# A recurrent-memory attention block: output and input projections in four column groups, transposes moved from TensorE to DMA

## The chip, the cores and the metric

The kernel runs on one core of a Trainium2 chip. The time is device time in microseconds (us) for one execution. The same kernel before the change, run on several chips, had medians from 5,003 to 5,043 us, so kernels of different batches are compared through their ratio to the kernel before of the same batch.

## The reference, cut to what matters

It is a forward and backward pass of one block. The attention half is recurrent: 64 segments of 32 rows run one after the other, each with 8 memory rows that the segment before produced.

```python
for s in range(n_seg):                         # 64 segments, serial
    xs = x[:, s*32:(s+1)*32]                   # 32 rows of 448
    h = concatenate([mem, xs])                 # 8 + 32 = 40 rows
    q, k, v = h@Wq, h@Wk, h@Wv                 # 448 -> 16 heads x 256 = 4096
    p = softmax(mask(q@k.T * scale))
    o = (p@v) @ Wo                             # 4096 -> 448
    mem = o[:, :8]                             # the only link to the next segment
    outs.append(o[:, 8:])
...
h  = x + attention(layernorm(x))
h2 = h + swiglu_ffn(layernorm(h))              # 448 -> 1792 -> 448
# outputs: h2 and the gradients of x, mem0, Wq, Wk, Wv, Wo, w_gate, w_up, w_down
```

The gradient runs the same chain backwards. Only the 8 memory rows tie one segment to the next.

## The kernel before

It has five parts in order: the forward chain, the FFN forward and backward, the backward chain, the attention weight gradients, the FFN weight gradients. Instructions of the chains are issued at high priority; other work (called filler below) is placed by the scheduler into the waits of the chain. Each engine then executes its list in that fixed order, and what stands behind a waiting instruction waits as well: in run 3 four transposes that wait for their operand hold up TensorE 16 times, for 65.2 us in all.

In the chains, everything is kept with features on the partitions and the 40 rows of the segment as the moving operand, so every projection is 128 matmuls of 40 columns.

```python
def wpass(W_sb, s):                            # one of V, Q, K; three passes per segment
    for c in range(MC):                        # MC = 32
        for kc in range(KC):                   # KC = 4
            nc.tensor.matmul(o, lhsT=W_sb[:, kc, c*P:(c+1)*P], rhs=hT_roll[:, kc, sl, :], ...)   # 40 columns
# ... forward, output projection of all 40 rows:
for mc in range(KC):
    for c in range(MC):
        nc.tensor.matmul(pO[:, mc*L:(mc+1)*L], lhsT=Wo_sb[:, c, mc*P:(mc+1)*P], rhs=oT[:, c, :], ...)
# ... backward, 384 of them per segment:
for mc in range(KC):
    for (WT, dT) in ((WvT_sb, dvT), (WkT_sb, dkT), (WqT_sb, dqT)):
        for c in range(MC):
            nc.tensor.matmul(pH[0:msz, mc*L:(mc+1)*L], lhsT=WT[:, c, mcols], rhs=dT[:, c, :], ...)
# ... attention weight gradients: gather, then transpose on TensorE, then accumulate in SBUF
for j in range(8):
    nc.tensor.transpose(pt[:, j*P:(j+1)*P], stg[:, c, :], ident[:, :])
# ... cuts: softmax on 40x640, V and dO transposed on TensorE, end of each FFN tile:
nc.vector.tensor_copy(out=dh_b[:, 0:D], in_=dh_t[:])
for kc in range(KC):
    nc.tensor.transpose(pdT[:, kc*P:(kc+1)*P], dh_b[:, kc*P:(kc+1)*P], ident[:, :])
```

## Time and profile before

The median was 5,043.25 us of 16 runs (5,014.49 to 5,046.56). The first fence has lines from the page of the kernel before: the busy time of each engine with its share and instruction count, two rows of the 40 slices (granted TensorE clock in tenths, and DMA share in tenths), and the chain of work that ended last.

```profile
PE 3974.7 (79%) x94152; PEld 3396.5 (68%) x94192; DVE 2129.7 (42%) x4096; ACT 1577.5 (31%) x2696; POOL 397.4 (8%) x809
...
PEclk9888888888888788987888888888888898887979
DMA  5111111211211311115232322322233346465352
...
PE 64%; DVE 11%; ACT 8%; DMA 8%; issue 5%; SPq 2%; ACTq 0%; POOL 0%; DVEq 0%; POOLq 0%
```

TensorE holds 64% of the chain and issues 94,152 matmuls. DMA has room in the chains: its share is 0.17 and 0.30 in the next fence. The next fence is the table of windows of the kernel before, one row for each stretch: its length, then busy time and instruction count of each engine, granted clock, DMA share, GB/s.

```profile
56.00:1671.00 1615.00, 1290.21 (x41284) 1253.51 (x41285) 798.07 (x1506) 510.98 (x816) 90.34 (x236) 0.87 0.17 61
1671.00:2280.00 609.00, 404.14 (x2500) 230.31 (x2528) 308.22 (x560) 192.57 (x326) 43.04 (x103) 0.87 0.21 72
...
2343.00:3950.00 1607.00, 1425.91 (x44100) 1372.13 (x44096) 544.12 (x1105) 461.50 (x802) 157.52 (x305) 0.86 0.30 91
3950.00:4833.00 883.00, 686.36 (x5152) 442.29 (x5152) 444.20 (x843) 374.75 (x676) 69.80 (x128) 0.88 0.50 145
```

These are the forward chain (25.2 us per segment), the FFN, the backward chain (25.1 us per segment) and the attention weight gradients. Last, the timeline of TensorE in one forward segment: start, length, line, operands, count, and in brackets the idle time before with what ended it.

```profile
609.12 0.72 PE L505 MATMUL psh<-ident,P_sb 40*40 40x40 bf16 x16 [4.36 <-DVE P_sb L501]
...
611.72 3.98 PE L525 MATMUL psf<-oT,Wo_sb 128*128 128x40 bf16 x128
615.98 3.35 PE L367 MATMUL psf<-hT_roll,Wv_sb 128*128 128x40 bf16 x128 [0.28 <-DVE hT_roll L530]
```

A pass of 128 narrow matmuls takes 3.35 us, 26 ns each, and the chain pays for each of them.

### The profile page before, as it was taken

The page shows a single profiled execution, that of the slowest core. Times are in us where ns is not written, and L with a number is a line of the kernel's source. Part 1 is how long each engine was busy: PE and PEld are TensorE (multiplying, and loading weights), DVE is VectorE, ACT ScalarE, POOL GpSimd, SP SyncE. Part 2 cuts the span into 40 slices and gives each one's busy share as a digit, 9 for nine tenths or more (in the row PEclk, how much of TensorE's full clock was granted, in tenths as well). Part 3 has the DMA queues.
Part 4 walks back from the last instruction along what each step waited for, and adds up shares of the span by engine and source line. Part 5 has one row for each costly group of instructions (what it writes and reads, how often), then busy time and mean ns, then how long its engine had stood idle before and what let it go on. Part 6 is the DMA issues. An engine that isn't in the chain of part 4 may idle for free.

```text
span 5027.9 us, 201264 instructions
## 1 busy us (share of the span) xinstructions
PE 3974.7 (79%) x94152; PEld 3396.5 (68%) x94192; DVE 2129.7 (42%) x4096; ACT 1577.5 (31%) x2696; POOL 397.4 (8%) x809
## 2 busy tenths in 40 slices
PE   4788878877887577675898888888888787875949
PEld 3777777777777433344888888888888654543525
DVE  3445544544454455552333333333333363644520
ACT  2333333322333333232222222222222434433420
POOL 2000000000000100001011000100010100000000
PEclk9888888888888788987888888888888898887979
DMA  5111111211211311115232322322233346465352
GB/s 164 52 61 60 68 51 61 77 51 51 78 59 50 118 60 58 65 59 167 85 101 89 96 89 90 95 90 89 90 92 92 122 126 167 144 159 171 119 190 94
DMA packets 257044, 477.74 MB, mean 95 GB/s; under 512 B 95008, under 2 KB 145344, under 8 KB 246992
## 3 DMA queue, kind: packets, MB, share of 16 engines
q1 hardware_dynamic: 215872, 307.71, 19.6%
q0 software_dynamic: 40336, 157.14, 9.6%
q8 instruction: 737, 12.08, 1.0%
q14 instruction: 99, 0.81, 0.1%
HBM read 228.30 MB, written 219.13 MB: 89 GB/s over the span
## 4 chain that ended last, share of the span: by engine, by line
PE 64%; DVE 11%; ACT 8%; DMA 8%; issue 5%; SPq 2%; ACTq 0%; POOL 0%; DVEq 0%; POOLq 0%
PE psf L819 15%; PE psf L367 12%; PE psf L962 5%; PE psf L525 5%; PE psf L745 4%; ACT dO_sb L77 4%; PE psf L1015 2%; PE psf L1049 2%; PE psf L689 2%; SPq L978 1%; PE psh L923 1%; PE psf L756 1%; PE psf L797 1%; PE psf L620 1%; PE psf L806 1%
## 5 line engine op out<-in xcount | busy, mean ns | idle before, releaser
L962 PE MATMUL psf<-H_all,ktg 128*128 128x448 bf16 x1920 | 367.4, 354 | 5.8 <-ACT accT L77 5.8
L825 DVE CAST doutT_all<-psf 128x24 bf16<-128x24 f32 x63 | 11.5, 183 | 735.8 <-PE psf L819 735.8
L819 PE MATMUL psf<-dvT,WvT_sb 128*128 128x40 bf16 x8192 | 295.6, 191 | 22.2 <-issue 22.0
L962 PEld LDWEIGHTS <-ktg 128*128 128x128 bf16 x1920 | 188.0, 98 | 180.6 <-issue 8.5
L819 PE MATMUL psf<-dqT,WqT_sb 128*128 128x40 bf16 x8192 | 287.9, 188 | 21.7 <-issue 21.7
L819 PE MATMUL psf<-dkT,WkT_sb 128*128 128x40 bf16 x8192 | 290.2, 189 | 17.6 <-issue 17.4
L819 PEld LDWEIGHTS <-WvT_sb 128*128 128x128 bf16 x8192 | 269.1, 107 | 29.5 <-issue 24.2
L819 PEld LDWEIGHTS <-WqT_sb 128*128 128x128 bf16 x8192 | 264.3, 106 | 24.5 <-issue 24.0
L525 PE MATMUL psf<-oT,Wo_sb 128*128 128x40 bf16 x8192 | 274.3, 198 | 8.3 <-DVE oT L75 3.0
L819 PEld LDWEIGHTS <-WkT_sb 128*128 128x128 bf16 x8192 | 266.5, 106 | 20.3 <-issue 20.0
L525 PEld LDWEIGHTS <-Wo_sb 128*128 128x128 bf16 x8192 | 271.1, 109 | 12.0 <-DVE oT L75 4.2
L77 ACT COPY dO_sb<-psh 40x1024 bf16<-40x1024 bf16 x256 | 238.6, 1007 | 107.5 <-PE psh L776 107.5
L923 PE MATMUL psh<-ident,kstg 128*128 128x128 bf16 x2048 | 160.2, 252 | 131.8 <-DVE kstg L915 131.8
L832 ACT COPY dxnT_tile<-psf 128x96 f32<-128x96 f32 x64 | 15.3, 239 | 778.4 <-DVE doutT_all L826 767.1
L923 PEld LDWEIGHTS <-kstg 128*128 128x128 bf16 x2048 | 151.0, 116 | 141.6 <-DVE kstg L915 139.0
L745 PE MATMUL psf<-doutT_all,WoT_sb 128*128 128x40 bf16 x8192 | 224.2, 182 | 13.1 <-DVE doutT_all L825 13.1
L745 PEld LDWEIGHTS <-WoT_sb 128*128 128x128 bf16 x8192 | 224.3, 98 | 14.0 <-issue 12.0
L367 PE MATMUL psf<-hT_roll,Wk_sb 128*128 128x40 bf16 x8192 | 222.3, 179 | 13.9 <-issue 13.0
L367 PEld LDWEIGHTS <-Wv_sb 128*128 128x128 bf16 x8192 | 216.4, 96 | 17.8 <-issue 17.6
L367 PE MATMUL psf<-hT_roll,Wv_sb 128*128 128x40 bf16 x8192 | 217.5, 180 | 13.5 <-DVE hT_roll L530 13.5
L505 PE MATMUL psh<-ident,P_sb 40*40 40x40 bf16 x1024 | 41.3, 188 | 234.7 <-DVE P_sb L501 234.7
L367 PEld LDWEIGHTS <-Wk_sb 128*128 128x128 bf16 x8192 | 212.4, 96 | 18.4 <-issue 18.0
(293 smaller groups left out, 7224.1 us busy)
## 6 DMA issues: line engine op xcount, KB each, us to landing
VT_all<-vT SPq DMA_DIRECT2D x64, 320.0 KB, 2.2
OT_all<-oT POOLq DMA_DIRECT2D x64, 320.0 KB, 2.8
vT_b<-VT_all SPq DMA_DIRECT2D x64, 320.0 KB, 2.9
dVT_all<-dvT SPq DMA_DIRECT2D x64, 320.0 KB, 2.7
dKT_all<-dkT POOLq DMA_DIRECT2D x64, 320.0 KB, 4.1
dQT_all<-dqT SPq DMA_DIRECT2D x64, 320.0 KB, 4.4
Kx<-tmq SPq DMA_DIRECT2D x64, 256.0 KB, 2.4
Qx<-tmq SPq DMA_DIRECT2D x64, 256.0 KB, 2.4
```

The costliest lines, as they stand in the source:

```text
L77: nc.scalar.copy(out=out, in_=in_)
L367: nc.tensor.matmul(o, lhsT=W_sb[:, kc, c * P:(c + 1) * P], rhs=hT_roll[:, kc, sl, :], start=(kc == 0), stop=(kc == KC - 1))
L525: nc.tensor.matmul(pO[:, mc * L:(mc + 1) * L], lhsT=Wo_sb[:, c, mc * P:(mc + 1) * P], rhs=oT[:, c, :], start=(c == 0), stop=(c == MC - 1))
L620: nc.tensor.matmul(pg[:, 0:f1 - f0], lhsT=hnT[:, kc, :], rhs=Wg_sb[:, kc, f0:f1], start=(kc == 0), stop=(kc == KC - 1))
L689: nc.tensor.matmul(pdh[:, 0:D], lhsT=srcT[:, c, :], rhs=WT[:, c, :], start=(i == 0), stop=(i == nmm - 1))
L745: nc.tensor.matmul(o, lhsT=WoT_sb[:, kc, c * P:(c + 1) * P], rhs=doutT_all[:, kc, s, :], start=(kc == 0), stop=(kc == KC - 1))
L756: nc.tensor.matmul(pdP[b][0:L, hh, 0:L], lhsT=doT[:, c, :], rhs=vT[:, c, :], start=(dc == 0), stop=(dc == DC - 1))
L819: nc.tensor.matmul(pH[0:msz, mc * L:(mc + 1) * L], lhsT=WT[:, c, mcols], rhs=dT[:, c, :], start=(i == 0), stop=(i == 3 * MC - 1))
L923: nc.tensor.transpose(pt[:, j * P:(j + 1) * P], stg[:, c, :], ident[:, :])
L962: nc.tensor.matmul(pacc[:, 0:D], lhsT=KT_sb[:, sl, j * P:(j + 1) * P], rhs=H_all[:, kt, 0:D], start=(i == 0), stop=(i == len(slots) - 1))
L1015: nc.tensor.matmul(pacc[:, 0:D], lhsT=KT_sb[:, sl, mc * P:(mc + 1) * P], rhs=dOut_all[:, kt, :], start=(i == 0), stop=(i == len(slots) - 1))
L1049: nc.tensor.matmul(pacc[:, 0:f1 - f0], lhsT=HN_all[:, kt, mc * P:(mc + 1) * P], rhs=X_all[:, kt, f0:f1], start=(kt == 0), stop=(kt == NT - 1))
```

## The change: intent and diff

The intent is to issue fewer, wider matmuls on the chain. Only the 8 memory rows need the output projection at once; the other 32 rows can wait until four segments make a full 128-row tile. For the 8 rows the roles of the operands are swapped: the activations (32 columns, 8 of them real) are loaded as weights, and the weight matrix streams as 448 columns. Four such matmuls, each writing to its own 32 of the 128 rows of one PSUM tile (a column group), can run side by side. Small FP32 matmuls then add the four partial sums. Most transposes leave TensorE for the DMA (issued from SyncE, SP). Below is the core of the diff, long parts cut.

```diff
-            for mc in range(KC):
-                for c in range(MC):
-                    nc.tensor.matmul(pO[:, mc * L:(mc + 1) * L], lhsT=Wo_sb[:, c, mc * P:(mc + 1) * P],
-                                     rhs=oT[:, c, :], start=(c == 0), stop=(c == MC - 1))
+            pO = k.ps1()
+            for j in range(MC):
+                nc.tensor.matmul(pO[32 * (j % 4):32 * (j % 4) + 32, 0:D], lhsT=oTm[:, j, :], rhs=Wo_sb[:, cj(j), :],
+                                 start=(j < 4), stop=(j >= MC - 4), skip_group_check=True)
+            ...                                          # copy to om, FP32 sum of the four groups by 'sel'
+        if r == 3:                                       # filler: the other rows, once per 128-row tile
+            for j in range(MC):
+                nc.tensor.matmul(px[:, 0:D], lhsT=xblk[:, j, :], rhs=Wo_sb[:, cj(j), :], ...)
... V: x rows projected per tile as filler; the 8 memory rows in column groups on the chain, then copied into V
+            for j in range(4):
+                eng.dma_start(out=Vs[64 * g + SEG:64 * g + L, ...], in_=v_sb[32 * j:32 * j + M, :])
... backward: DMA transposes in place of TensorE's, three projections in column groups, the rest as filler (px)
+        nc.sync.dma_start_transpose(out=vT[...], in_=dr["VG"][s])      # also Q_sb, K_sb: 512 KB each
+            nc.sync.dma_start_transpose(out=dO_sb[:], in_=doT[...])    # on the chain
+                for j in range(MC):
+                    nc.tensor.matmul(pH[32 * (j % 4):32 * (j % 4) + 32, 0:D], lhsT=dm_pad[nm][:, j, :], rhs=WT[:, cj(j), :], ...)
... FFN: the transpose of dh at the end of a tile is gone; dh goes to DRAM and is transposed by DMA later
-        for kc in range(KC):
-            nc.tensor.transpose(pdT[:, kc * P:(kc + 1) * P], dh_b[:, kc * P:(kc + 1) * P], ident[:, :])
... attention weight gradients: transposed tiles by DMA, accumulation over 20 blocks in PSUM
+                    nc.sync.dma_start_transpose(out=x_t[...], in_=src)              # 256 KB each, 320 of them
```

## The prediction

> **What bounds it now.** TensorE, at its instruction rate. The page counts 94,152 matmuls and as many weight loads, PE busy 79% of 5028 us; in the chain of waits PE holds 64%. By the table of windows: prologue 0–56, forward chain 56–1671 (64 serial segments, 25.2 us each), FFN 1671–2280, weight loads to 2343, backward chain 2343–3950 (25.1 us per segment), attention weight gradients 3950–4833 (883 us), FFN weight gradients to 5028. In the timeline 128 matmuls of 40 columns take 3.36 us: 26 ns each. So the chains pay per matmul.
>
> **What changes.** About 53,500 matmuls remain.
> - Forward, per segment: the V pass (3.36 us) and V transposes (1.95) go; V is projected per 128-row tile off the chain, only the 8 memory rows on it (32 matmuls of 512 columns in four column groups). Output projection: 128 narrow matmuls (4.46 us) become 32 of 448 columns in four column groups, memory rows only. Softmax runs on 128x320 instead of 40x640 (0.81 us per op becomes about 0.45). New on the chain: four small SBUF-to-SBUF copies that put the memory rows into V (small DMAs here land in about 1.7–2.2 us), and four FP32 matmuls summing the column groups (about 0.7 us).
> - Backward, per segment: 384 matmuls of the three input projections (about 13.5 us) become 96 wide ones in column groups (about 2 us per 32); dO transposes on TensorE with four ACT copies (3.7 us) become one DMA transpose; 96 narrow head matmuls become 48. Added: four 512 KB DMA transposes per segment on the SP queue.
> - Attention weight gradients: the transposes (2,560 matmuls), the SBUF accumulations and the transposed write-back go; 320 DMA transposes of 256 KB feed PSUM accumulation over 20 blocks.
>
> Everything rests on column groups running concurrently.[...]
>
> **Sum (estimates from the durations above).** Forward segment: two passes 6.75, evacuation and scores 1.0, softmax and V evacuation 2.8, DMA 2.7, PV 1.2, projection 2.0, FP32 sum and copies 1.5: with semaphores 18.8 us. Backward segment: pass 3.95, scores and softmax 3.3, three rounds of about 3.1 us, sum and copies 1.5, filler 1.3: about 20 us; SP needs about 9 us of it for transposes, hidden. Weight gradients: 1,440 matmuls of 512 columns at 0.216, 480 in pairs, 640 of 448 at 0.19, plus bubbles: about 560 us. The SP queue issued 1 MB transposes every 4.2 us, so 84 MB takes about 355 us, hidden.
> 70 + 64x18.8 + 605 + 63 + 64x20 + 560 + 195 = about 3,980; with DMA contention I say 4,020 us, 8 in 10 between 3,750 and 4,400. Faster by over 2%: 0.94; within 2%: 0.02; slower: 0.04.
>
> **What would show each step.** 32 column-group matmuls spanning about 2 us (6–7 us if serial: then near 5,200 us and slower). Segments of 18–20 us forward, 19–21 backward. In the forward chain, the small V copies as the releaser before PV. In the gradient stretch PE, not SP, as limiter; 30–35 us per quarter.
>
> **What would make it wrong.** Column groups serialising; the small V copies waiting behind the 512 KB stores of Q, K, V; DMA transposes of 256–512 KB slower than the 1 MB ones, making the SP queue the limit in the backward chain or the gradients.

A speed-up was assumed for four column groups; no trace showed it at the time. No term is missing from the sum, which came to about 3,980 us, and 4,020 with contention, but the terms of about 2 us for 32 column-group matmuls rest on that assumption: the projection's 2.0 us forward and the three backward rounds, 3.1 us each with their other parts. From the trace of before one can only bound them: matmuls of 448 columns start 189 ns apart, so 32 take 6.0 us one after the other and 1.5 us if four run wholly side by side (estimates). The changed kernel and run 2 give the answer: 1.70 us in four groups, 6.23 in one. The pairing of 480 matmuls in the weight gradients was assumed too; in the changed kernel the second of a pair starts 3 to 4 ns after the first (L887). Two smaller estimates: the softmax operations on VectorE came out at 0.49 us ("about 0.45"), and the FP32 sum on TensorE, with filler between, at 1.26 us from start to end ("about 0.7"; medians).

## The result and the profile after

The changed kernel took 4,024.46 us (median of 9 runs, 4,015.51 to 4,049.9) against 5,043.25 us; the ratio is 0.7991, 95% interval 0.7974 to 0.8007. The predicted 4,020 us is nearly exact, but the stretches show that this is in part luck. First the page of the changed kernel, the lines that answer to those shown of before.

```profile
PE 3314.0 (82%) x54269; PEld 2086.0 (52%) x54366; DVE 1413.6 (35%) x3195; ACT 871.7 (22%) x2021; POOL 816.8 (20%) x1733
...
PEclk9999989999998799886899999999999888999979
DMA  7334334333333312218788888868887799999852
```

The matmuls fell to 54,269, and DMA is now busy: the backward chain and the attention weight gradients are at 8 and 9 tenths. (The chain of work that ended last covers only 10% of this trace, so it is not used for the changed kernel.) The table of windows of the changed kernel, stretch for stretch:

```profile
57.00:1306.00 1249.00, 1104.57 (x26011) 798.19 (x26066) 510.13 (x1153) 331.42 (x782) 235.85 (x535) 0.93 0.39 142
1306.00:1838.00 532.00, 385.03 (x2412) 223.81 (x2440) 294.74 (x548) 182.67 (x317) 49.13 (x119) 0.89 0.22 80
...
1906.00:3164.00 1258.00, 1155.12 (x22522) 752.74 (x22521) 484.40 (x1216) 271.66 (x783) 369.48 (x824) 0.95 0.81 168
3164.00:3834.00 670.00, 526.76 (x2594) 237.85 (x2592) 99.80 (x230) 72.40 (x111) 125.23 (x201) 0.89 1.03 193
```

| stretch (us) | before | predicted | after |
|---|---|---|---|
| prologue | 56 | 70 | 57 |
| forward chain, 64 segments | 1,615 | 1,203 | 1,249 |
| FFN | 609 | 605 | 532 |
| weight loads | 63 | 63 | 68 |
| backward chain, 64 segments | 1,607 | 1,280 | 1,258 |
| attention weight gradients | 883 | 560 | 670 |
| FFN weight gradients | 195 | 195 | 197 |

The chains gave 715 of the 997 us saved between the two profiled runs (366 forward, 349 backward). The attention weight gradients gave 213 where 323 were expected; the FFN gave 77 where 4 were. The timeline of TensorE in two neighbouring forward segments of the changed kernel shows what the main part of the gain looks like, and something the prediction did not have:

```profile
917.04 1.23 PE L451 MATMUL psf<-PT_bd,V 128*128 128x80 bf16 x16 [2.20 <-DMA V<-v_sb]
918.20 2.67 PE L461 MATMUL psf<-Wo_sb,oTm 128*32 128x448 bf16 x32
...
934.36 2.44 PE L493 MATMUL fx<-Wo_sb,xblk 128*128 128x448 bf16 x12
936.64 0.74 PE L451 MATMUL psf<-PT_bd,V 128*128 128x80 bf16 x16
937.44 1.70 PE L461 MATMUL psf<-Wo_sb,oTm 128*32 128x448 bf16 x32
```

L461 is the projection in column groups: 32 matmuls of 448 columns (a set, below) in 1.70 us. In the trace the four matmuls of a round start within 11 ns of each other, and the rounds 0.18 to 0.19 us apart. L451 is the product of the probabilities and V (PV, below). In the segment before, where TensorE stood idle for 2.20 us first, the same 32 took 2.67 us; where filler (L493) ran instead, they took 1.70. L451 shows the same, 1.23 against 0.74. The windows of the two sets show the granted clock, third figure from the end:

```profile
918.20:920.87 2.67, 2.67 (x35) 1.11 (x34) 0.69 (x2) 0.79 (x3) 0.94 (x2) 0.62 0.77 308
937.44:939.14 1.70, 1.70 (x33) 0.84 (x34) 0.72 (x2) 0.79 (x3) 0.94 (x2) 1.00 0.67 258
```

In segments 1 to 62 of the forward chain it was 1.00 in each of the 37 sets that took 1.70 us, and 0.50 to 0.64 in each of the 25 that took longer.

What TensorE waited for in the changed kernel, from the list of waits (total us, times, longest):

```profile
PE psf L883 <- ACT wres L77: 58.3, 9, 31.2
PE psf L714 <- DMA dO_sb<-doT: 56.5, 17, 7.5
...
PE psf L451 <- DMA V<-v_sb: 44.4, 25, 2.2
```

Apart from one of the FFN that the kernel before has as well (58.3 us, 16 times, for VectorE's dgp), these are the three largest waits that recur: evacuations (copies of TensorE's results out of their PSUM tiles) in the attention weight gradients, the transpose of dO (the gradient of PV's result) in the backward chain, the copies of V's memory rows in the forward chain. Each was tried.

### The profile page after: what moved, and what is told of

It reads as the page before. It is cut to its first block, busy times and chain, and to the rows that moved or that the text cites. A ratio compares the mean times of both kernels' runs of the same rounds, so it can differ in the third digit from the quotient of the medians.

```text
span 4031.1 us, 121412 instructions
## 1 busy us (share of the span) xinstructions
PE 3314.0 (82%) x54269; PEld 2086.0 (52%) x54366; DVE 1413.6 (35%) x3195; ACT 871.7 (22%) x2021; POOL 816.8 (20%) x1733
## 5 line engine op out<-in xcount | busy, mean ns | idle before, releaser
L883 PE MATMUL psf<-xt,HC 128*128 128x512 bf16 x1440 | 349.6, 405 | 112.7 <-ACT wres L77 58.3
L883 PEld LDWEIGHTS <-HC 128*128 128x128 bf16 x1440 | 146.9, 103 | 314.2 <-issue 167.4
L723 PE MATMUL psf<-do_roll,WoT_sb 128*128 128x40 bf16 x8192 | 218.4, 180 | 74.1 <-POOL do_roll L683 72.3
L379 PEld LDWEIGHTS <-Wq_sb 128*128 128x128 bf16 x8192 | 228.9, 99 | 19.6 <-issue 8.2
L379 PE MATMUL psf<-hT_roll,Wq_sb 128*128 128x40 bf16 x8192 | 229.5, 184 | 6.6 <-DVE hT_roll L473 5.3
L414 PE MATMUL psf<-Wv_sb,memT_pad 128*32 128x512 bf16 x2048 | 147.7, 381 | 0.4 <-issue 0.3
L461 PE MATMUL psf<-Wo_sb,oTm 128*32 128x448 bf16 x2048 | 142.0, 433 | 2.9 <-DVE oTm L75 0.4
L794 PE MATMUL fx<-WqT_sb,blkq 128*128 128x448 bf16 x512 | 128.5, 365 | 0.0
L794 PE MATMUL fx<-WvT_sb,blkv 128*128 128x448 bf16 x512 | 127.8, 369 | 0.0
L842 DVE COPY mpk<-mld 128x1024 bf16<-128x1024 bf16 x32 | 13.4, 434 | 324.9 <-DMA xt<-mpk 277.6
L794 PE MATMUL fx<-WkT_sb,blkk 128*128 128x448 bf16 x512 | 124.6, 354 | 0.0
```

Of the source, the lines that this page charges most:

```text
L379: nc.tensor.matmul(pss[b][:, jj * L:(jj + 1) * L], lhsT=W_sb[:, kc, c * P:(c + 1) * P], rhs=hT_roll[:, kc, sl, :], start=(kc == 0), stop=( ...
L414: nc.tensor.matmul(pV[b][32 * j:32 * j + 32, 0:512], lhsT=memT_pad[:, kc, :], rhs=Wv_sb[:, kc, n * 512:(n + 1) * 512], start=(kc == 0), st ...
L461: nc.tensor.matmul(pO[32 * (j % 4):32 * (j % 4) + 32, 0:D], lhsT=oTm[:, j, :], rhs=Wo_sb[:, cj(j), :], start=(j < 4), stop=(j >= MC - 4), ...
L723: nc.tensor.matmul(pss[b][:, jj * L:(jj + 1) * L], lhsT=WoT_sb[:, kc, c * P:(c + 1) * P], rhs=do_roll[:, kc, sl, :], start=(kc == 0), stop ...
L794: nc.tensor.matmul(px[:, 0:D], lhsT=blk[nm][:, j, :], rhs=WT[:, cj(j), :], start=(wi == 0 and j == 0), stop=(wi == 2 and j == MC - 1))
L883: nc.tensor.matmul(pa[2 * kc + g][:, 0:512], lhsT=HC[:, b, kc * P:(kc + 1) * P], rhs=xt[b][:, :, g, :], start=(b == 0), stop=(b == NB - 1))
```

## The experiments

Twelve kernels were run, in four batches with the kernel before in each. In the traces of the experiments the forward stretch is counted to the first TensorE instruction of the FFN, because that is easy to find in every trace; so counted it is 1,274 us in the changed kernel, 25 us more than in the table above. For parts of the kernel that an experiment left untouched, the stretches repeat from trace to trace within these limits (seven traces or more each): forward 1,271 to 1,278 us, backward 1,226 to 1,258, attention weight gradients 654 to 684. A difference inside such limits shows nothing.

### 1. Column groups one after the other, first attempt

```diff
-            for j in range(MC):
+            for j in sorted(range(MC), key=lambda j: (j % 4, j)):      # also in the backward chain
```

> The changed kernel, but the 32 matmuls of the memory-row projections (one projection forward, three backward, per segment) are issued one column group after the other instead of going round the four groups. Same count, same shapes, same sums. My theory: the gain comes from four column groups running at once; 32 matmuls, now 1.70 us in the trace, then span about 6 us[...], +4.3 us four times in each of 64 segments, so about +1,100 us and a time near 5,100 us. Rival: what counts is only that 128 or 96 narrow matmuls became 32 wide ones (fewer instructions); then the order is indifferent and the time stays within 1% of 4,024 us.

It took 4,542.13 us, ratio 0.9053 (0.899 to 0.9116), correct. So the order of the groups alone is worth about half of the gain. But a set spanned 4.00 us, not 6.0 (32 times the 189 ns from start to start in the kernel before), at the same granted clock of 1.00. From the trace: in one set, the first four and the last four matmuls start 0.189 us apart, those between start in pairs, the second of a pair 0.005 to 0.017 us after the first. Two groups still ran side by side, so the experiment did not do quite what it was meant to.

### 2. All 32 matmuls in one column group

```diff
-                nc.tensor.matmul(pO[32 * (j % 4):32 * (j % 4) + 32, 0:D], ...
-                                 start=(j < 4), stop=(j >= MC - 4), ...)
+                nc.tensor.matmul(pO[0:32, 0:D], ...
+                                 start=(j == 0), stop=(j == MC - 1), ...)
... the same for pH in the backward chain; only om[0:32] is copied, the other rows stay zero
```

> All 32 memory-row matmuls of a set (one set forward, three backward per segment) add into column group 0 alone, so no two of them can run side by side; the order question of the first attempt is gone and the result stays correct. Theory (the column groups run concurrently, and this is what pays for the change): each set spans [...]6.0 us instead of 1.70, 4.3 us per segment forward and 12.9 backward, 64 segments: +1,100 us, about 5,120 us, ratio 1.02 to the kernel before, so the whole gain is gone. Rival (the 4.00 us of the first attempt was already serial, and the rest was accumulation into one bank): 4.0 us per set again, about 4,540 us.

It took 5,069.33 us, ratio 1.0091 (1.0047 to 1.0135), correct. The timelines of TensorE, one line of the first attempt and one of this kernel, are:

```profile
903.84 4.00 PE L461 MATMUL psf<-Wo_sb,oTm 128*32 128x448 bf16 x32
```

```profile
901.84 6.23 PE L461 MATMUL psf<-Wo_sb,oTm 128*32 128x448 bf16 x32
```

With little else changed (the copies of the sums read 32 rows instead of 128), 32 matmuls take 6.23 us in one group and 1.70 us in four, both at a granted clock of 1.00: 3.7 times. In one group they start 189 ns apart, as the full-width matmuls of 448 columns in the changed kernel do, so adding up in one place costs nothing extra. The forward stretch grew by 285 us and the backward stretch by 750, and the whole kernel is no faster than the kernel before. The theory holds: without concurrency of the column groups the change gains nothing in sum. Counted as in the table above, the forward chain would be about 1,534 us (1,615 before) and the backward chain 2,008 (1,607); the other parts keep their gains. The rival (4.0 us was already serial) is out.

### 3. The FFN's transposes put back

The FFN gained 77 us though the change only drops four transposes per tile there.

```diff
+        pdT = ps1(BF16)
+        for kc in range(KC):
+            nc.tensor.transpose(pdT[:, kc * P:(kc + 1) * P], dh_b[:, kc * P:(kc + 1) * P], ident[:, :])
+        dhT = work.tile([P, KC, P], BF16, name="dhT", bufs=1)
+        k.evac(dhT[:], pdT[:, 0:KC * P].rearrange("p (c n) -> p c n", n=P))
```

> The changed kernel, with the four TensorE transposes of the layer-norm gradient put back at the end of each of the 16 FFN tiles (and their copy out of PSUM, into a scratch tile nobody reads). Theory: in the FFN the in-order TensorE waited 4.1 us per tile for the vector chain that ends in this tile (61 us in the trace of before); the FFN stretch goes from 532 back to about 600 us, the time from 4,024 to about 4,090 us. Rival: the FFN gained for another reason (its loads, its PSUM pool, the strided copy into the persistent gradient tile); then only the work itself comes back, 64 short matmuls, 7 us, and the time stays under 4,040 us.

It took 4,076.31 us, ratio 0.8136 (0.8096 to 0.8176), correct; the FFN stretch grew by 61 us. The waits of TensorE, the line in the kernel before and the line that came back:

```profile
PE psh L701 <- DVE dh_b L697: 65.3, 16, 4.1
```

```profile
PE psh L652 <- DVE dh_b L647: 65.2, 16, 4.1
```

The four transposes need dh, the last result of VectorE's chain of layer-norm operations. In TensorE's fixed order they stood before the next tile's matmuls and held them up to 4.1 us, 16 times. Once they start, the four take 0.40 us in this trace, so nearly all of the 61 us is the wait, not the work.

### 4. Filler taken out of the forward chain

```diff
-            for j in range(MC):
-                nc.tensor.matmul(px[:, 0:D], lhsT=xblk[:, j, :], rhs=Wo_sb[:, cj(j), :], start=(j == 0), stop=(j == MC - 1))
+            for j in range(1):
+                nc.tensor.matmul(px[:, 0:D], lhsT=xblk[:, j, :], rhs=Wo_sb[:, cj(j), :], start=True, stop=True)
```

> Wrong on purpose: the forward output projection per 128 rows, which runs between the chain's matmuls on the same in-order engine, is cut from 32 matmuls of 448 columns to 1, 16 times in the forward stretch (96 us of PE work over all: 31 x 0.19 x 16). Theory (fillers stretch the serial chain, because a chain matmul that becomes ready must wait for the filler already in the queue): the forward stretch loses 40 to 96 us of its 1,249. Rival (fillers sit in waits of the chain and are free): under 15 us.

It is wrong; the comparison with the reference accepted it all the same, so that comparison vouches for nothing in this part. It took 4,048.48 us, ratio 0.8057 (0.8027 to 0.8088). Both theory and rival fell: with 496 matmuls fewer the forward stretch became 30 us longer (1,304). The timeline of this kernel:

```profile
935.05 0.37 PE L443 MATMUL psf<-ident,P_sb 128*40 128x40 bf16 x16 [1.59 <-DVE P_sb L439]
937.52 1.07 PE L451 MATMUL psf<-PT_bd,V 128*128 128x80 bf16 x16 [2.10 <-DMA V<-v_sb]
938.52 2.97 PE L461 MATMUL psf<-Wo_sb,oTm 128*32 128x448 bf16 x32
```

Without filler TensorE idles for 1.59 us, works for 0.4, idles for 2.10, and then the column groups take 2.97 us. The granted clock of the forward stretch fell from about 0.94 to between 0.86 and 0.90. The changed kernel shows the same link. In its slowest sets the granted clock was 0.50, and they took 3.18 us against 1.70, 1.87 times as long. Its clock record has 200 spells of 1.00 or 0.50, with nothing between, and each but the last is a multiple of 3.41 us long. In the 5 us before a set TensorE was busy with matmuls for 29% of the time where the set was slow (median of 25, 24 to 60%) and for 92% where it took 1.70 us (median of 37, 56 to 96%). In the timeline above two gaps of 1.59 and 2.10 us, with 0.37 us of work between them, come before the slow set. How much idle time brings the clock down was not measured; whether the idle time is the cause is what the next run asks.

### 5. Unneeded matmuls added to two of four segments

```diff
+            if r >= 2:
+                pz = k.fx1()
+                for i in range(4):      # in the wait for the softmax; 7 more in the wait for V
+                    nc.tensor.matmul(pz[0:64, 0:512], lhsT=qT[:, i, :], rhs=Wv_sb[:, 0, 0:512], start=True, stop=True)
```

> Adds work that nothing needs: in two of every four forward segments (the ones that get no or few filler matmuls) 4 matmuls of 512 columns in the wait for the softmax and 7 in the wait for the copies of V, 0.9 and 1.5 us, into a PSUM bank nobody reads; the result stays correct. Theory (in segments without filler TensorE idles about 4 us of 4.5 before PV, its clock falls to half, and the 32 column-group matmuls then take 2.6 to 3.2 us instead of 1.70 and the next pass 7.4 instead of 6.6; this also explains why taking filler away made the forward stretch 30 us longer): the slow sets become 1.70 us, the mean granted clock of the stretch rises from 0.94, and the stretch of 1,274 us loses 20 to 50 us. Rival (the slow sets have another cause, for example DMA traffic of those segments): the sets stay slow and the stretch grows by up to 30 us from the added work.

It took 3,995.52 us, ratio 0.7988 (0.7967 to 0.801), correct: no gain over the changed kernel. The forward stretch was 1,267 us against 1,274. The set that took 2.67 us at 918.20 us above is now:

```profile
919.86 1.70 PE L469 MATMUL psf<-Wo_sb,oTm 128*32 128x448 bf16 x32
```

The clock theory is confirmed, the size of the gain is not. I measured the span of every column-group set in the forward chain (segments 1 to 62 of 0 to 63), counted those over 2 us by the segment's place in its tile of four, and took the mean time per segment:

| kernel | sets over 2 us, places 0, 1, 2, 3 | mean set | mean segment |
|---|---|---|---|
| changed kernel | 0, 2, 8, 15 | 2.21 us | 19.20 us |
| filler taken out (4) | 2, 12, 16, 15 | 2.65 us | 19.76 us |
| work added, places 2 and 3 (5) | 0, 2, 0, 0 | 1.74 us | 19.13 us |
| work added, place 3 only (12) | 0, 3, 16, 0 | 2.08 us | 19.79 us |

Adding work removed all but two of the slow sets and raised the granted clock of the forward stretch to 0.97 to 0.98. The set got 0.47 us shorter, the segment only 0.07: the steps around it grew. From the start of the FP32 sum to the first pass it took 0.24 us longer, from PV to the set 0.15, the passes 0.09. In the order of the compiled instructions, real filler now stands at those places, since the added work took its place in the waits.

### 6. The copies of V's memory rows off the chain

```diff
+    V_scr = wf.tile([P, 2048], BF16, name="V_scr")
-                eng.dma_start(out=Vs[64 * g + SEG:64 * g + L, ...], in_=v_sb[32 * j:32 * j + M, :])
+                eng.dma_start(out=V_scr[64 * g + SEG:64 * g + L, ...], in_=v_sb[32 * j:32 * j + M, :])
```

> Wrong on purpose: the four small copies of the memory rows of V go to a scratch tile that nothing reads, so PV no longer waits for them; all other work is the same. Theory (the copies, about 3.2 us from issue to landing, bound the forward segment, as the prediction put 2.7 us of DMA on the chain): PE's waits for V before PV (44 us by the copy, 67 with P) go away and the forward stretch loses 45 to 100 us. Rival (the softmax and P-transpose path and the filler matmuls end at about the same time, so the copies are hidden): under 20 us.

Its output is wrong, which doesn't matter for the time. It took 3,975.12 us, ratio 0.7913 (0.7862 to 0.7965). The forward stretch lost 56 us (1,218), inside the theory's range and far outside the 7 us by which untouched forward stretches differ. The median step from the transposed probabilities to PV fell from 2.21 to 1.03 us. So the copies, 16 KB each, cost the forward chain about 0.9 us per segment. It is their time to landing that counts: in the segment of the changed kernel shown above, PV starts 3.4 us after the first is issued (913.63 to 917.04 us). (Slow sets fell from 25 to 13 as well and the mean set to 1.95 us, but the steps after it grew by about as much.)

### 7. Stores of the backward chain moved to later segments

In the backward chain 26 of 62 segments take 17.0 us, and 22 take 20.0 to 29.6. In about two thirds of the slow ones TensorE waits for the dO transpose. The suspects were three 1 MB stores per 128-row tile that GpSimd issues a few us earlier.

```diff
-                nc.gpsimd.dma_start(out=dr["X_" + nm][t], in_=blk[nm][:]...)     # three at once, at r == 0
+            late = [(t, nm, blk[nm]) for nm in "kvq"]                            # one in each following segment
```

> The changed kernel; in the backward chain the three 1 MB stores that end every fourth segment are issued one per segment, over the next three segments. Same bytes. Theory: the burst of 3 MB takes the DMA engines from the transposes of Q, K and dO that stand in order on the SP queue (K took 8.5 us to issue after a burst, 2.3 us otherwise), so dO comes late and TensorE waits (56 us for dO, 25 us for vT in all). Spread out, the slow segments (20 to 29 us) become 17 to 20: the time falls by 40 to 70 us. Rival: the delay comes from the SP queue's own order (K's transpose has to wait for its only buffer, and dO stands behind it), whatever the stores do; then the waits stay above 60 us and the time within 15 us of 4,024.

It took 4,031.53 us, ratio 0.8037 (0.7993 to 0.8081), correct, and the backward stretch was 1,254 us: no gain. But the trace shows that the edit had not worked: the three stores were issued at 2,045, 2,050 and 2,055 us, all inside one segment, because nothing held the later ones back. It neither confirms nor refutes.

### 8. The same stores, held back

```diff
+        if late and r != 2:
+            lt, lnm, lb = late.pop(0)
+            nc.gpsimd.dma_start(out=dr["X_" + lnm][lt][0:1, 0:M], in_=x8[0:1, 0, :])   # waits for this segment's result
+            nc.gpsimd.dma_start(out=dr["X_" + lnm][lt], in_=lb[:]...)                  # must follow the tiny store
```

> The earlier attempt at spreading the three 1 MB stores of the backward chain did not spread them: the trace shows them 5 us apart, still in the slow segment. Here each store must wait for a tiny store of that segment's result to the same place, so one falls in each of three segments of four, none in the segment with the extra transpose. Theory (the slow backward segment, 21 to 29 us against 17.0, comes from the stores crowding the 256-byte transposes of dO, vT, Q and K): the slow segments shrink to 18 to 20 us, the wait for dO falls from 56 us below 25, and the backward stretch of 1,258 us loses 40 to 90 us. Rival (the extra transpose and the order of the queue alone make it): a slow segment of 21 us or more in every four remains, gain under 20 us.

It took 4,049.31 us, ratio 0.8092 (0.8075 to 0.8109), correct, 1% slower than the changed kernel by its ratio. TensorE's wait for dO rose from 56.5 to 104.8 us and from 17 times to 32; the backward stretch was 1,283 us. The expected gain is out, yet the trace tells what a store does. The next fence is the timeline of SP's queue in this kernel (start, time until the next could be issued).

```profile
2179.40 1.60 SPq L730 DMA_TRANSPOSE dO_sb<-doT  x1
...
2200.12 1.23 SPq L680 DMA_TRANSPOSE dhx<-DHb  x1
2201.45 3.97 SPq L730 DMA_TRANSPOSE dO_sb<-doT  x1
...
2220.68 5.14 SPq L730 DMA_TRANSPOSE dO_sb<-doT  x1
```

GpSimd issued stores at 2,198.0 and 2,219.5 us, each within 4 us before a dO transpose, and those two took 3.97 and 5.14 us; the one at 2,179.40 had no store near it, took 1.60, and its segment took 17.0 us. The segments with a store took 24.3 and 20.1 us. In the whole chain of this kernel, the 30 dO transposes with a store issued in the 4 us before took 3.99 us in the median, the other 34 took 1.67; TensorE waited in 22 segments of the first kind and 10 of the second. So a store just ahead of the chain's transpose goes with a delay, and tying the store to the end of a segment put it there. But it does not explain the changed kernel: there none of the 64 dO transposes has a store issued in the 4 us before (the nearest are 4.6 us or more), and 29 take over 2 us all the same, up to 9.39. What slows those is not shown.

The segment of 24.3 us also has the transpose of dh (L680) ahead of dO. SP's waits in the changed kernel, from 1,960 to 3,160 us, show that its own 1.2 us may be the smaller part:

```profile
SPq L680 <- POOL do_roll L683: 78.6, 13, 8.8
```

SP stood at this transpose for 78.6 us in all, until GpSimd had copied out the previous tile, and dO came behind it in the same queue. How much of that delayed the chain is not shown by this (run 12 tried to find out).

### 9. dO transposed on TensorE again

```diff
-            nc.sync.dma_start_transpose(out=dO_sb[:], in_=doT[:]...)
+            for hf in range(2):
+                pdo = k.ps1b()
+                for c8 in range(8):
+                    nc.tensor.transpose(pdo[:, c8 * P:(c8 + 1) * P], doT[...], ident[:, :])
+                k.evac(dO_sb[:, 8 * hf:8 * hf + 8, :], pdo[:, 0:1024]..., "s")
```

> dO is transposed on TensorE again (16 transposes of 128x128 and two ACT copies of 128x1024 per segment) in place of the 512 KB DMA transpose on the SP queue. Theory (the slow segments of the backward chain, 21 to 29 us against 17, come from the dO transpose standing behind others on the SP queue and the crowded DMA): PE no longer waits for dO (56 us, 17 times), slow segments shrink, backward stretch loses 40 to 60 us in spite of about 1 us more PE work per segment. Rival (the slow segments have another cause, the vT, Q and K transposes or the fillers): the waits move to vT, Q and K, backward stretch the same or up to 60 us longer from the added PE and ACT work.

It took 4,019.22 us, ratio 0.8003 (0.7969 to 0.8038), correct; backward stretch 1,256 us against 1,258. The wait for dO is gone from the list, but the time is the same. The windows of 1,960 to 3,100 us, in the changed kernel and then in this one:

```profile
1960.00:3100.00 1140.00, 1046.88 (x20710) 683.63 (x20710) 446.56 (x1123) 250.61 (x723) 342.82 (x764) 0.95 0.83 172
```

```profile
1960.00:3100.00 1140.00, 1091.58 (x21644) 716.82 (x21637) 446.97 (x1120) 367.01 (x838) 343.05 (x764) 0.98 0.66 145
```

TensorE was busy for 45 us more in the same 1,140 us, 96% of it. In the changed kernel a segment of 17.0 us holds 22 filler matmuls and 0.1 us of idle time. With the transposes back, only 17 fit, and four segments must place 96. The rest mostly fell on two segments of each tile, with 27 to 34 fillers and 19 to 24 us (two near 30). So the DMA transpose of dO saves TensorE work and costs waits of about equal size.

### 10. Packing copies of the weight gradients done quarter by quarter

In the attention weight gradients, TensorE waits for PSUM to be evacuated by ScalarE (58.3 us), while ScalarE and VectorE wait in turn (249.3 and 277.6 us) to repack memory-row gradients (the mpk tiles) until an earlier DMA transpose has read the buffer.

```diff
-                ld = work.tile([P, 16, 32, M], BF16, name="mld", bufs=1)
+                ld = work.tile([P, 16, 32, M], BF16, name="mld", bufs=4)
-                    pk = work.tile([P, 8, 16, M], BF16, name="mpk", bufs=20)      # all four quarters at once
+                pk = work.tile([P, 8, 16, M], BF16, name="mpk", bufs=8)           # one quarter, when it is needed
```

> The changed kernel; in the gradient stretch the copies that pack the memory-row blocks are made one quarter at a time, just before the quarter that uses them, instead of all 16 of a weight ahead of its first quarter. Same bytes, same DMA transposes, same matmuls. Theory: ScalarE and VectorE are in-order, a packing copy for the next weight waits for a buffer that a DMA transpose must free, and the PSUM evacuations stand behind it; so TensorE waits (ACT 58 us, DVE 22 us in the trace). Without it the quarters go from about 38 us to 33-34 and the first weight loses its 31 us gap: the stretch 670 becomes 580-610 us, the time about 3,950 us. Rival: the stretch is limited by the rate of the DMA transposes (DMA share 1.03 there); then the quarters stay at 37-38 us and the time within 10 us of 4,024.

It took 3,998.31 us, ratio 0.7967 (0.7928 to 0.8007), correct; the stretch was 655 us, inside the limits of untouched ones. The wait did not go: TensorE waited 86.2 us for ScalarE's evacuations, up to 42.7 us at once. In the timeline of ScalarE its copy at 3,310.19 had waited 39.11 us for a transpose with evacuations behind it. Eight buffers only moved the same queueing.

### 11. A full second set of packing buffers

```diff
-                    pk = work.tile([P, 8, 16, M], BF16, name="mpk", bufs=20)
+                    pk = work.tile([P, 8, 16, M], BF16, name="mpk", bufs=32)
-                    x_t = big.tile([P, 4, 2, P], BF16, name="xt", bufs=44)
+                    x_t = big.tile([P, 4, 2, P], BF16, name="xt", bufs=32)
```

> One change of sizes in the attention weight gradients: 32 buffers for the packed memory gradients in place of 20, paid for by 32 instead of 44 buffers for transposed tiles. Theory (the evacuations of PSUM stand on VectorE and ScalarE behind packing copies that wait for the DMA transposes to release a packing buffer; in the changed kernel TensorE waits 58 us for ScalarE and 22 us for VectorE there): with a full second set of buffers the copies never wait, those two waits fall below 20 us together, the stretch of 667 us loses 40 to 70 us. Rival (the DMA transposes are the limit in that stretch, its DMA share is 1.0, and the wait only moves): the wait for transposed tiles grows by as much, the stretch loses less than 20 us.

It took 3,975.04 us, ratio 0.7957 (0.7927 to 0.7987), correct; the stretch was 638 us, 16 below the lowest untouched one. TensorE's waits in this stretch, this kernel:

```profile
PE psf L883 <- DMA xt<-X_v: 40.2, 16, 7.7
PE psh L827 <- DVE hstg L824: 29.3, 4, 22.0
PE psf L883 <- DMA xt<-X_k: 22.5, 12, 7.4
PE psf L883 <- DMA xt<-mpk: 11.1, 8, 3.6
```

The waits for evacuations (58.3 and 22.3 us in the changed kernel) are gone, as the theory said. The waits for DMA transposes rose from 32 to 80 us (with 5.8 for X_q, not shown), as the rival said. All waits of TensorE in the stretch together fell from 140 to 109 us. Both were right in part: the evacuations hid a limit of nearly the same height. The timeline of SP in the changed kernel shows that limit, sixteen 256 KB transposes to a line:

```profile
3164.45 61.82 SPq L865 DMA_TRANSPOSE xt<-X_v  x16
...
3290.69 33.74 SPq L865 DMA_TRANSPOSE xt<-X_v  x16
```

The second line, with 2.6 us of waiting for TensorE in it, is 4.19 MB in 33.74 us, 124 GB/s, at a DMA share of 1.05 (the window of 3,290 to 3,325 us). The transposes go in 256-byte packets, median 18 ns each, 25 ns in the mean here, and share the engines with loads that this stretch started: all traffic of the window came to 209 GB/s.

### 12. Three changes together

```diff
+            if r == 3:                                                      # the added work of 5, place 3 only
-        hx_t = work.tile([P, KC, P], BF16, name="dhx", bufs=1)
+        hx_t = work.tile([P, KC, P], BF16, name="dhx", bufs=2)              # against SP's wait shown in 8
... buffers as in 11
```

> Three changes, each in another stretch, so that one trace can tell them apart; the result stays correct. (a) Forward: the 4 and 7 unneeded matmuls only in every fourth segment, the one that has no filler at all, so that no real filler is displaced: its column-group set takes 1.70 us instead of 2.6 to 3.2; stretch 1,274 us to 1,240 to 1,260 (if the gain is given back as before: 1,270). (b) Backward: two buffers instead of one for the transposed tile of dh (and one small result tile shares a buffer to make room). Theory: the slow segment of four comes from that transpose standing first in the SP queue, waiting for GpSimd's copies out of its only buffer (SP waited 78.6 us there, 13 times) with the dO transpose behind it: this wait goes, the stretch of 1,258 us (1,232 to 1,258 in other runs) loses 40 to 60 us. Rival (the stores alone make the slow segments, by slowing the dO transpose): SP's wait goes but the stretch stays above 1,225. (c) Attention weight gradients: 32 and 32 buffers as tested before, about 638 us instead of 667. Together about 3,900 to 3,950 us, ratio 0.775 to 0.787.

It took 4,040.21 us (median of 5), ratio 0.8022 (0.7994 to 0.8051), correct: no better than the changed kernel. (The traced run was the slowest of the five, 4,074.51 us.) All three parts missed, and the first tells most. (a) The forward stretch grew to 1,309 us. The table under 5 shows why the clock did not help: place 3 became fast, and place 2 slow, all 16 times. In the trace, the place without filler moved from 3 to 2: matmuls of the V projection in place 2 fell from 78 to none, in place 3 they rose from 5 to 201. The likely reason, read from the order of the program and not tested, is that the added matmuls take their PSUM buffers before the later V projection does, so that filler could no longer be brought forward into place 2. (b) SP's wait for GpSimd's copies stayed at 70.7 us (12 times). The scheduler used the second buffer to start the transpose one tile further ahead, and it waited at the same place. So the share of that wait in the slow segments was not tested and stays open. The backward stretch was 1,272 us. (c) The gradient stretch was 659 us, with 95 us of TensorE waiting for transposes (57.8 for X_v, 15.9 for X_k, 14.7 for mpk, 6.6 for X_q). The 638 us of run 11 did not repeat, so the gain of run 11 is not shown.

No version that gives a right result was shown to beat the changed kernel. Run 11 has the best ratio among the correct ones, with an interval that overlaps the changed kernel's.

## Why the prediction was right or wrong

**Right: TensorE bound the chains, and column groups pay for the change.** The set spans 1.70 us at a granted clock of 1.00 ("about 2 us" was predicted), 6.23 us in one group ("6–7 us if serial: then near 5,200 us"; 5,069 measured). Run 2 shows this directly. "At its instruction rate" was not tested by a run of its own, but the trace of before supports it: successive matmuls of 448 columns start 189 ns apart there, and those of 40 columns 25 ns, where the columns alone would make 17 (an estimate from the 189).

**Right: the segments.** 18–20 us forward were predicted and 19.2 measured; 19–21 backward, and 19.3. But the parts differ. Forward, "DMA 2.7" for the copies of V was in the sum and run 6 shows that they do bound PV. "Projection 2.0" came out at 2.21 in the mean, made up of 1.70 where filler runs and up to 3.18 where it does not. Backward, the sum of 20 us was reached in another way: 26 of 62 segments take 17.0, below the predicted range, and 22 take 20.0 to 29.6.

**Wrong: "SP needs about 9 us of it for transposes, hidden".** In the backward chain the dO transpose is on the chain, and TensorE waited for it 56.5 us. So "hidden" is what failed. In run 8 a 1 MB store issued just ahead goes with 3.99 us for it in place of 1.67 (medians); what delays it in the changed kernel, where no store comes that close, stays open.

**Wrong: the FFN term, 605 us; measured 532.** The prediction copied the stretch of before, though the diff removes the four transposes at the end of each tile. Their wait was in the list of waits of before: 65.3 us. Run 3 puts 61 us back.

**Wrong: the attention weight gradients, 560 us; measured 670.** The failed term is "84 MB takes about 355 us, hidden", which took the rate of quiet 1 MB transposes. "PE, not SP, as limiter; 30–35 us per quarter" failed for the first quarters: their sixteen X_v transposes alone took 62, 50, 34 and 37 us. In all, SP's queue was at the 320 transposes for 639 us by its timeline, with 96 us of waiting in them by its list of waits. Even the quickest four in a row, 1 MB together, took 5.3 us, where a 1 MB transpose took 4.2 in the kernel before: the prediction had named this among the things that would make it wrong. The 1,440 matmuls of 512 columns, put at 0.216 us each, kept TensorE busy for 349.6 us, 243 ns each, at a granted clock of 0.89 in that stretch; 216 ns is the median from start to start. Run 11 shows the second limit behind the first: with the evacuation waits gone, waits for transposes take most of their place. How much a faster feed would give in all was not tested.

The wrong sizes of the weight gradients and the FFN (+110 and −73) and the two chains (+46 and −22) cancel to within 61 us; the 40 us added for contention covers most of that.

**Not in the prediction: the clock.** The granted clock of the kernel before was 0.86 to 0.88 in its chains and was read as a given. It depends on the schedule: runs 4, 5 and 12 move the slow sets with the filler, and each slow set measured in the changed kernel had a granted clock of 0.50 to 0.64.

## What to carry to other kernels

A narrow matmul on a serial chain can cost more than its columns (25 ns for 40 of them here, where 189 ns for 448 would make 17). Swapping the operands pays only with the packing: 128 narrow matmuls took 3.35 us, the 32 wide ones 1.70 in four column groups and 6.23 in one; test it by putting all pieces in one group. Filler in the waits of a serial chain kept the granted clock up here (about 0.94 in the forward stretch; without 496 filler matmuls 0.86 to 0.90, and the stretch was 30 us longer), so count TensorE work removed from a wait as possibly negative gain, and look at where the filler lands after every change of buffers or priorities. When a wait ends at a busy engine or queue, ask what stands in front of the awaited instruction and which limit comes next; removing the first wait in the weight gradients mostly uncovered the second.
